# An mLSTM cell with hash routing: the gate prologue in three groups on 32 partitions, with the first rows moved inside SBUF

## The chip, the cores and the metric

The kernel runs on one core of a Trainium2 chip. The metric is the device time of one execution in microseconds; 429.63 us is the median of three runs before the change (429.09 to 429.99). The profile comes from one profiled execution with a span of 427.9 us.

The engines are named as the profile names them: PE (TensorE, with PEld for its weight loads), DVE (VectorE), ACT (ScalarE), POOL (GpSimd) and SP (SyncE). SPq and ACTq are the queues from which SyncE and ScalarE issue DMA transfers; both issue in program order.

## The reference: what is computed

Two blocks follow each other. The first is an mLSTM cell over 4 batches, 8 heads, 768 positions and head size 40. Cut to what matters:

```python
for t in range(S):
    m_new  = np.maximum(f_gate[:, :, t] + m, i_gate[:, :, t])
    f_stab = np.exp(f_gate[:, :, t] + m - m_new)
    i_stab = np.exp(i_gate[:, :, t] - m_new)
    m = m_new
    C = f_stab * C + i_stab * outer(v_t, k_t)
    n = f_stab * n + i_stab * k_t
    h = C @ q_t
    y[:, :, t] = sigmoid(o_gate[:, :, t]) * h / max(abs(n @ q_t), 1)
```

The second sends each of the 3072 rows of width 320 to one of 8 experts by a hash of its token id, and applies `relu(x @ w1[e]) @ w2[e]` with 1024 hidden columns.

## The kernel before

The cell is computed in chunks of P = 128 positions: 24 steps `s`, six per batch (`c = s % 6`), each for all 8 heads of a batch. Within a chunk the gates become decays `exp(A_t + e_u)`, where `A` is a running sum of log decays and `e` belongs to the input position. Those sums are formed on TensorE: `L` holds the rows of `e` and `R` the rows of `A`, each split into three bf16 pieces so that their sum has fp32 precision, and one product of the two gives the matrix that is then exponentiated.

```python
def decays(s):                      # PE, then ACT
    R = Rs[s % 2]
    for hf in range(2):
        for i in range(2):
            nc.tensor.matmul(ab[...], lhsT=Ls[b % 2][...], rhs=R[:, i, hf::2, :], ...)
        nc.scalar.activation(w[:, hf], ab[:], AF.Exp)

def weigh(s):                       # DVE: w = scores * decays
    for hf in range(2):
        nc.vector.tensor_tensor(d["w"][:, hf], d["sp"][hf][:], d["w"][:, hf], op=ALU.mult)
```

The prologue computes the gates of all 32 (batch, head) rows. It does so in two groups: `g0` is the first 256 positions on partitions 0 to 31; `g1` is the other 512 positions, folded to 256 columns on partitions 64 to 127. The gates of `g1` are loaded a second time in that layout, and the running maximum `m` is moved over to it by two transfers inside SBUF.

```python
def gates(rows, m0, m1, f, i, eng):
    nc.vector.tensor_add(aP[r], f, m0)
    nc.vector.tensor_sub(aP[r], aP[r], m1)
    nc.gpsimd.tensor_tensor(iP[r], i, m1, op=ALU.subtract)
    nc.vector.tensor_tensor_scan(AP[r], keep[r], aP[r], 0.0, op0=ALU.mult, op1=ALU.add)
    nc.vector.tensor_tensor(r1[r], AP[r], hi(AP[r]), op=ALU.subtract)
    nc.vector.tensor_sub(iP[r], iP[r], AP[r])
    nc.vector.tensor_tensor(r2[r], r1[r], hi(r1[r]), op=ALU.subtract)
    pieces_of(zA, 0, AP, r1, r2, r, eng)      # three bf16 copies
def gates_e(rows, eng): ...                   # r3, r4, three pieces of e into zE
def gates_rest(rows, eng): ...                # aP, exp(A), exp(aP), r1, r2, three more pieces
```

`zA` and `zE` are written to DRAM (`za_d`, `ze_d`), and `load_a(s)` and `load_e(b, groups)` read the rows that a step needs back into `R` and `L`, one head beside the other. `gates_turn` transposes `exp(aP)` into `kw_T`, the factors for the keys. The order of the prologue, cut:

```python
load_k(0); load_q0(0); load_k(1); load_q0(1); load_v(0); load_k(2)
...                                            # four more gate loads on ACT's queue
tables()                                       # constant parts of R and L
scan of m (g0); turn_k(0); turn_q0(0)
load_q0(2); load_o(0); load_v(1); load_o(1); load_v(2); load_o(2)
scores(0)
gates(g0, ...); gates_e(g0, ...); store_a(g0, A); store_e(g0, A)
turn_k(1); turn_q0(1)
scan of m (g1), two transfers of m to the layout of g1
load_a(0, A); load_e(0, [0])
gates_rest(g0, ...); store_x(g0, A)
Rs[1] <- Rs[0]                                 # two transfers, 128 and 256 KB
memsets of v on POOL
load_q(1, 0); load_q(1, 1)                     # batch 1's q, 2 x 480 KB
gates_turn(g0); decays(0); entering(0); load_a(1, A); k_weights(0)
gates(g1, ...); weigh(0); load_k(3); load_q0(3)
gates_e(g1, ...); store_a, store_e; gates_rest(g1, ...); store_x
...
```

Then the 24 steps. Every engine takes its work in this order:

```python
for s in range(NT):
    load_k(s + 3) (and load_q0(c + 3) in batch 0); load_v(s + 3)
    load_q(b + 2, ...) in chunks 2 and 4; load_o(...); a slice of the experts' weights
    decayed(s)                                 # POOL: C * decay
    turn_k(s + 2); turn_q0(c + 2) / turn_q(b + 1, r, ...)      # PE, evacuated by ACT
    back(s - 1); finish(s - 1)                 # PE, DVE, POOL
    decays(s + 1)
    if s == 0: load_e(0, [1, 2])
    sigmoid(s) in some steps                   # ACT
    state(s); entering(s + 1)                  # PE, DVE: C, qs
    load_a(s + 2, nc.scalar if s == 0 else nc.sync)
    k_weights(s + 1); store of x(s - 1)
    scores(s + 1); weigh(s + 1)
    pad_q(...)                                 # DVE
    for piece in before.get(s, []): piece()    # routing constants and the like
    attend(s)                                  # PE, evacuated by ACT
    if s == 0: sigmoid(0); gates_turn(g1)
    for piece in after.get(s, []): piece()
```

`turn_q` spreads the transposes of the next batch's q over the steps; `first_turns = {1: (0,), 2: (1,), 3: (2,), 4: (3, 4), 5: (5,)}` says which falls into which step of batch 0. `before[0]` holds three iotas with their casts on POOL, `before[1]` the other five. After the steps the rows are gathered from DRAM by expert, and the two layers follow.

Of the kernel before, what the change touches and what calls it, by code (L numbers as in the profile page):

```python
# [8 lines left out]
F32 = mybir.dt.float32  # L9
# [8 lines left out]
P = 128  # L18
NEG = -1e30
# [3 lines left out]
def kernel(  # L23
# [90 lines left out]
    za_d = nc.dram_tensor("decay_pieces", (3 * BH, 6, 2 * P), BF16, kind="Internal").ap()  # L114
    ze_d = nc.dram_tensor("input_pieces", (3 * BH, 3, 2 * P), BF16, kind="Internal").ap()

    with tc.tile_pool(name="gates", bufs=1) as gp, \
# [24 lines left out]
        at = [0, 2 * BH, 3 * BH]  # L142
        fP, iP, aP, AP, r1, r2, r3, r4 = (
            gp.tile([P, W2], F32, name=name) for name in ("fP", "iP", "aP", "AP", "r1", "r2", "r3", "r4")
        )
        mP = gp.tile([P, W2 + 1], F32, name="mP")
        keep = gp.tile([P, W2], F32, name="keep")
        zA = gp.tile([P, 6, W2], BF16, name="zA")
        zE = gp.tile([P, 3, W2], BF16, name="zE")
# [36 lines left out]
        def load_e(b, gs):  # L186
            src = ze_d.rearrange("(g b h) i t -> b (h i) g t", g=NC2, h=H)[b]
            nc.scalar.dma_start(
                Ls[b % 2][: 3 * H, :].rearrange("r (g t) -> r g t", t=W2)[:, gs[0] : gs[-1] + 1],
                src[:, gs[0] : gs[-1] + 1],  # L190
            )

        def load_a(s, eng):
            b, c = s // NB, s % NB
            r0 = c // 2 * BH + b * H
            n = 3 if c == 0 else 6
            src = za_d[r0 : r0 + H, :n, c % 2 * P : (c % 2 + 1) * P].rearrange("h i t -> i h t")
            for i in range(2):
                eng.dma_start(Rs[s % 2][32 : 32 + n, i], src)
# [5 lines left out]
        def pieces_of(z, i0, t, ra, rb, r, eng):  # L205
            for j, piece in enumerate((hi(t[r]), hi(ra[r]), rb[r])):
                if eng[j] is nc.scalar:
                    nc.scalar.copy(z[r, i0 + j, :], piece)
                else:
                    nc.gpsimd.tensor_copy(z[r, i0 + j, :], piece)  # L210

        def gates(rows, m0, m1, f, i, eng):

            r = rows
            first = r.start == 0
            nc.vector.tensor_add(aP[r], f, m0)
            nc.vector.tensor_sub(aP[r], aP[r], m1)
            if first:
                nc.vector.memset(aP[r, 0:1], 0.0)
            nc.gpsimd.tensor_tensor(iP[r], i, m1, op=ALU.subtract)  # L220
            nc.vector.tensor_tensor_scan(AP[r], keep[r], aP[r], 0.0, op0=ALU.mult, op1=ALU.add)
            nc.vector.tensor_tensor(r1[r], AP[r], hi(AP[r]), op=ALU.subtract)
            nc.vector.tensor_sub(iP[r], iP[r], AP[r])
            nc.vector.tensor_tensor(r2[r], r1[r], hi(r1[r]), op=ALU.subtract)
            pieces_of(zA, 0, AP, r1, r2, r, eng)

        def z_rows(r):
            return slice(0, BH) if r.start == 0 else slice(BH, 3 * BH)

        def gates_e(rows, eng):  # L230
            r = rows
            nc.vector.tensor_tensor(r3[r], iP[r], hi(iP[r]), op=ALU.subtract)
            nc.vector.tensor_tensor(r4[r], r3[r], hi(r3[r]), op=ALU.subtract)
            pieces_of(zE, 0, iP, r3, r4, r, eng)

        def store_a(r, eng):
            eng.dma_start(za_d[z_rows(r), :3, :], zA[r, :3, :])

        def store_e(r, eng):
            eng.dma_start(ze_d[z_rows(r)], zE[r])  # L240

        def store_x(r, eng):
            eng.dma_start(za_d[z_rows(r), 3:, :], zA[r, 3:, :])

        def gates_rest(rows, eng):
            r = rows
            Ac = AP[r].rearrange("p (c t) -> p c t", t=P)
            n = r.stop - r.start
            nc.vector.tensor_tensor(
                aP[r].rearrange("p (c t) -> p c t", t=P), iP[r].rearrange("p (c t) -> p c t", t=P),  # L250
                Ac[:, :, P - 1 : P].to_broadcast([n, 2, P]), op=ALU.add,
            )
            nc.scalar.activation(fP[r], AP[r], AF.Exp)
            nc.scalar.activation(aP[r], aP[r], AF.Exp)
            nc.vector.tensor_tensor(r1[r], fP[r], hi(fP[r]), op=ALU.subtract)
            nc.vector.tensor_tensor(r2[r], r1[r], hi(r1[r]), op=ALU.subtract)
            pieces_of(zA, 3, fP, r1, r2, r, eng)

        def gates_turn(rows):
            r = rows  # L260
            n = r.stop - r.start
            tp = ps.tile([P, 2, n], F32, name="tpg", tag="tr", bufs=4)
            for c in range(2):
                nc.tensor.transpose(tp[:, c, :], aP[r, c * P : (c + 1) * P], ident[r, r])
            lo, hi_ = (0, 1) if r.start == 0 else (1, 3)
            nc.vector.tensor_copy(
                kw_T[:, :, lo:hi_, :].rearrange("p c g n -> p c (g n)"), tp[:],
            )
# [325 lines left out]
        def route_index():  # L594
# [7 lines left out]


        before = {
            0: [lambda: iota_consts(0, 3)], 1: [lambda: iota_consts(3, 8)], 2: [route_consts, route_sel],
# [4 lines left out]
        after = {4: [route_counts], **{13 + i: [lambda i=i: route_table(i)] for i in range(NT // TH)}}  # L610
# [3 lines left out]
        first_turns = {1: (0,), 2: (1,), 3: (2,), 4: (3, 4), 5: (5,)}  # L614
# [26 lines left out]
        flat = {id(t): src.rearrange("b h s -> (b h) s") for t, src in ((f_sb, f_gate), (i_sb, i_gate), (fP, f_gate), (iP, i_gate))}  # L641
        nc.scalar.dma_start(f_sb[:], flat[id(f_sb)])
        nc.scalar.dma_start(i_sb[:], flat[id(i_sb)])
# [9 lines left out]
        for i in (1, 2):  # L653
            for t in (fP, iP):
                nc.scalar.dma_start(t[at[i] : at[i] + BH, :], flat[id(t)][:, i * W2 : (i + 1) * W2])
        nc.vector.memset(m_sb[:, 0:1], 0.0)
        tables()
        for t in [ks[2], kws[0]]:
            nc.gpsimd.memset(t[:, :, D:], 0.0)
        nc.vector.memset(keep[:], 1.0)  # L660
        nc.vector.memset(keep.rearrange("p (c t) -> p c t", t=P)[:, :, 0:1], 0.0)
        g0, g1 = slice(0, BH), slice(2 * BH, 4 * BH)
        A, G = nc.scalar, nc.gpsimd
        nc.vector.tensor_tensor_scan(
            m_sb[:, 1 : W2 + 1], f_sb[:, :W2], i_sb[:, :W2], NEG, op0=ALU.add, op1=ALU.max,
        )
        turn_k(0)
        turn_q0(0)
        load_q0(2)
        load_o(0)  # L670
        load_v(1)
        load_o(1)
        load_v(2)
        load_o(2)
        scores(0)
        gates(g0, m_sb[:, :W2], m_sb[:, 1 : W2 + 1], f_sb[:, :W2], i_sb[:, :W2], (G, G, G))
        gates_e(g0, (A, A, A))
        store_a(g0, A)
        store_e(g0, A)
        turn_k(1)  # L680
        turn_q0(1)
        nc.vector.tensor_tensor_scan(
# [310 lines left out]
```

## Time and profile before

| | |
|---|---|
| time, median of three runs | 429.63 us |
| span of the profiled run | 427.9 us |
| PE busy | 386.1 us (90%) |
| DVE, ACT, POOL busy | 136.1, 134.6, 118.7 us |
| DMA moved | 51.37 MB, mean 120 GB/s |
| the 24 steps end (last attend) | at about 164 us |

The profile page gives busy time per engine, the span in 40 slices with a digit for the busy share (9 is 90% or more), the clock that TensorE was granted, the share of the DMA engines, and the chain of work that ended last. Other views give the same trace by stretches of time, by waits (who waited for whom), and in order of time. A wait with several causes is put down to the one that came last. In a line of the timeline or of the chain the first number is the start in us and the second the length.

### The profile page before, as it was taken

The page shows a single profiled execution, that of the slowest core. Times are in us where ns is not written, and L with a number is a line of the kernel's source. Part 1 is how long each engine was busy: PE and PEld are TensorE (multiplying, and loading weights), DVE is VectorE, ACT ScalarE, POOL GpSimd, SP SyncE. Part 2 cuts the span into 40 slices and gives each one's busy share as a digit, 9 for nine tenths or more (in the row PEclk, how much of TensorE's full clock was granted, in tenths as well). Part 3 has the DMA queues.
Part 4 walks back from the last instruction along what each step waited for, and adds up shares of the span by engine and source line. Part 5 has one row for each costly group of instructions (what it writes and reads, how often), then busy time and mean ns, then how long its engine had stood idle before and what let it go on. Part 6 is the DMA issues. An engine that isn't in the chain of part 4 may idle for free.

```text
span 427.9 us, 7402 instructions
## 1 busy us (share of the span) xinstructions
PE 386.1 (90%) x2862; PEld 258.5 (60%) x2862; DVE 136.1 (32%) x371; ACT 134.6 (31%) x238; POOL 118.7 (28%) x204
## 2 busy tenths in 40 slices
PE   2369999999999992599999999999999999999992
PEld 2257867877887871356656557556556566575551
DVE  7464748766675761211020120110110210201100
ACT  5158776686495471011010110110111111111010
POOL 6363323313323422710321501302302312021021
PEclk9868999999999998589999999999999999999997
DMA  8929998899676720527616318235216201000000
GB/s 168 213 61 172 206 218 180 190 205 214 149 161 129 161 90 33 163 96 239 193 46 212 120 29 271 62 98 170 75 64 214 61 8 38 0 15 31 1 17 30
DMA packets 111784, 51.37 MB, mean 120 GB/s; under 512 B 86624, under 2 KB 105892, under 8 KB 111748
## 3 DMA queue, kind: packets, MB, share of 16 engines
q1 hardware_dynamic: 105898, 39.31, 38.2%
q0 software_dynamic: 2496, 8.20, 6.0%
q10 hardware_dynamic: 3354, 3.37, 2.4%
q8 instruction: 23, 0.38, 0.4%
q14 instruction: 13, 0.11, 0.1%
HBM read 42.00 MB, written 8.63 MB: 118 GB/s over the span
## 4 chain that ended last, share of the span: by engine, by line
PE 78%; issue 5%; ACT 5%; DMA 4%; POOL 2%; DVE 1%; SPq 1%; ACTq 0%; POOLq 0%; DVEq 0%
PE mh L834 22%; PE zp L863 21%; PE mh L827 6%; PE sp L351 6%; PE ht L409 6%; PE ht L402 3%; PE ab L311 2%; PE tr L275 2%; PE xo L424 2%; PE ht L382 2%; PE tk L588 1%; PE tp L810 1%; ACT qT L289 1%; PE xb L323 1%; PE tr L288 1%
## 5 line engine op out<-in xcount | busy, mean ns | idle before, releaser
L863 PE MATMUL zp<-w2t,h 128*128 128x320 f32 x384 | 105.2, 433 | 0.0
L834 PE MATMUL mh<-xT,w1t 128*128 128x416 f32 x256 | 98.9, 531 | 0.9 <-POOL xT L896 0.9
L863 PEld LDWEIGHTS zp<-w2t,h 128*128 128x128 f32 x384 | 72.7, 190 | 32.1 <-issue 3.3
L834 PEld LDWEIGHTS mh<-xT,w1t 128*128 128x128 f32 x256 | 47.8, 194 | 44.0 <-issue 41.6
L816 DVE COPY xT<-tp 128x384 f32<-128x384 f32 x16 | 8.9, 558 | 142.3 <-PE tp L812 124.7
L797 POOL DMA_INDIRECT out_dram<-zo,s_idx x26 | 25.6, 986 | 92.5 <-ACT zo L796 92.5
L843 ACT ACTIVATE h<-mh 128x416 f32<-128x416 f32 x32 | 16.6, 517 | 110.1 <-PE mh L827 60.3
L796 ACT COPY zo<-zp 128x320 f32<-128x320 f32 x26 | 11.1, 426 | 101.1 <-PE zp L863 92.9
L841 DVE TENSOR_SCALAR h<-mh 128x416 f32<-128x416 f32 x32 | 18.9, 592 | 53.4 <-PE mh L834 26.9
L359 DVE TENSOR_TENSOR w<-sp,w 128x512 f32<-128x512 f32 x48 | 30.9, 686 | 13.8 <-PE sp L351 10.3
L440 POOL TENSOR_TENSOR x<-x,den 128x320 f32<-128x320 f32 x24 | 17.4, 724 | 64.0 <-DVE den L439 34.1
L351 PE MATMUL sp<-qT,kT 64*128 64x128 f32 x384 | 29.7, 297 | 4.1 <-ACT qT L289 4.1
L351 PEld LDWEIGHTS sp<-qT,kT 64*128 64x128 f32 x384 | 24.9, 199 | 10.8 <-ACT qT L289 6.0
L315 ACT ACTIVATE w<-ab 128x512 f32<-128x512 f32 x48 | 26.6, 611 | 5.0 <-PE ab L311 4.9
L409 PE MATMUL ht<-w,v 128*64 128x128 f32 x384 | 27.1, 285 | 0.0
L827 PE MATMUL mh<-xT,w1c 64*128 64x416 f32 x128 | 26.7, 535 | 0.0
L938 POOL COPY hrem<-h 128x256 f32<-128x256 f32 x8 | 3.2, 400 | 84.1 <-ACT h L843 84.1
L790 POOL DMA_INDIRECT xg<-x_rows,g_idx x24 | 23.4, 976 | 9.7 <-issue 9.7
L417 ACT COPY hT<-ht 128x512 f32<-128x512 f32 x24 | 14.1, 587 | 31.2 <-PE ht L409 31.2
L409 PEld LDWEIGHTS ht<-w,v 128*64 128x64 f32 x384 | 21.2, 140 | 4.0 <-issue 3.1
L289 ACT COPY qT<-tr 128x512 f32<-128x512 f32 x24 | 22.9, 975 | 0.6 <-PE tr L288 0.3
L275 PE MATMUL tr<-ident,k 128*128 128x128 f32 x96 | 17.2, 307 | 4.3 <-DMA k<-in_k_dram 4.3
(177 smaller groups left out, 407.0 us busy)
## 6 DMA issues: line engine op xcount, KB each, us to landing
w2t<-in_moe_w_dram SPq DMA_DIRECT2D x28, 320.0 KB
w1t<-in_moe_w_dram SPq DMA_DIRECT2D x28, 256.0 KB
k<-in_k_dram SPq DMA_DIRECT2D x24, 160.0 KB
v<-in_v_dram SPq DMA_DIRECT2D x24, 160.0 KB
og<-in_o_gate_dram SPq DMA_DIRECT2D x24, 160.0 KB
x_rows<-x SPq DMA_DIRECT2D x24, 160.0 KB
ql<-in_q_dram SPq DMA_DIRECT2D x6, 480.0 KB
w1c<-in_moe_w_dram SPq DMA_DIRECT2D x14, 128.0 KB
```

What stands on the lines that cost most here:

```text
L275: nc.tensor.transpose(tp[:, j, :], d["k"][:, 2 * j : 2 * j + 2, :].rearrange("p h d -> p (h d)"), ident[:])
L289: nc.scalar.copy(qb[b]["T"][:, :, cols], tp[:])
L315: nc.scalar.activation(w[:, hf], ab[:], AF.Exp)
L351: nc.tensor.matmul(sp[hf][:, j, :], lhsT=d["kT"][r, j, :], rhs=q_of(s)[r, j, :], start=True, stop=True,)
L359: nc.vector.tensor_tensor(d["w"][:, hf], d["sp"][hf][:], d["w"][:, hf], op=ALU.mult)
L409: nc.tensor.matmul(place(j, hf), lhsT=d["v"][:, 2 * j + hf, :], rhs=d["w"][:, hf, j, :], start=(c == 0 and j0 == 0), stop=True, skip_group ...
L790: nc.gpsimd.indirect_dma_start(out=xg, out_offset=None, in_=x_d[:, :], in_offset=bass.IndirectOffsetOnAxis(ap=idx, axis=0),)
L797: ins = nc.gpsimd.indirect_dma_start(out=out[:, :], out_offset=bass.IndirectOffsetOnAxis(ap=idx, axis=0), in_=zo[:], in_offset=None, bound ...
L827: nc.tensor.matmul(hp[i][:, :cols], lhsT=w1c[r, fp, :], rhs=xT[r, 2, :cols], start=first, stop=not first,)
L834: nc.tensor.matmul(hp[i][:, :cols], lhsT=w1t[:, db, fb * P : (fb + 1) * P], rhs=xT[:, db, :cols], start=(first and db == 0), stop=(not fir ...
L841: nc.vector.tensor_relu(h[:, 2 * fp, :cols], hp[i][:, :cols])
L863: nc.tensor.matmul(zp[:], lhsT=h[:, fb, j * P : (j + 1) * P], rhs=w[2][:, fb, :], start=(fb == 0), stop=(fb == FB - 1),)
```

## The change

The prologue is rewritten. The gates are now computed in three groups of 256 positions, all on partitions 0 to 31, so that neither the second load of the gates nor the transfers of `m` are needed. The rows of the first step do not go through DRAM: `zA` and `zE` are moved by nine small transfers straight into `R` and `L`. The second group's work stands partly in the prologue and partly in step 0, the third group's in steps 0 to 2, with its exponents and stores behind the evacuations of those steps. Fourteen spare products (`spin`) stand in TensorE's order in the prologue. Loads of `o` and of batch 1's q move to later places, and the first turns of batch 1's q begin a step later. The purpose is an earlier start of the steps. The diff, cut to its core:

```diff
-        fP, iP, aP, AP, r1, r2, r3, r4 = (gp.tile([P, W2], ...) ...)
+        fP, iP, AP, r1, r2, r3, r4 = (gp.tile([BH, W2], ...) ...)
+        aP = [gp.tile([BH, W2], F32, name=f"aP{i}") for i in range(2)]
-        zA = gp.tile([P, 6, W2], BF16, name="zA")
-        zE = gp.tile([P, 3, W2], BF16, name="zE")
+        zA = gp.tile([BH, 6, S], BF16, name="zA")
+        zE = gp.tile([BH, 3, S], BF16, name="zE")
 ...
+        def gates_m(g):     # scan of m for group g (DVE)
+        def gates_a(g):     # two DVE, iP on POOL, scan of A (DVE)
+        def gates_b(g, eng):  # five DVE, six pieces: zA on POOL, zE on eng
+        def gates_end(g):   # one DVE
+        def gates_exp(g, end):  # ACT: exp(aP) if end, else exp(A)
+        def gates_x(g):     # two DVE, three pieces on POOL
+        def store_a(g, eng):  # all six rows of zA;  store_e: three of zE
+        def spin(n):
+            t = ps.tile([P, 2, 512], F32, name="ht")
+            for _ in range(n):
+                nc.tensor.matmul(t[:, 1, :P], lhsT=ident[:], rhs=ident[:], start=True, stop=True)
 ...
+        def gates_last():
+            gates_exp(2, True)
+            gates_x(2)
+            store_a(2, nc.sync)
+            store_e(2, nc.sync)
         before = {
-            0: [lambda: iota_consts(0, 3)], 1: [lambda: iota_consts(3, 8)], 2: [...],
+            0: [lambda: gates_m(2), lambda: gates_a(2), lambda: iota_consts(0, 3)],
+            1: [lambda: gates_b(2, G), lambda: gates_end(2), lambda: iota_consts(3, 8)], 2: [...],
-        after = {4: [route_counts], ...}
+        after = {1: [gates_last], 4: [route_counts], ...}
-        first_turns = {1: (0,), 2: (1,), 3: (2,), 4: (3, 4), 5: (5,)}
+        first_turns = {2: (0,), 3: (1,), 4: (2, 3), 5: (4, 5)}
 ...
-        for i in (1, 2):
-            for t in (fP, iP):
-                nc.scalar.dma_start(t[at[i] : at[i] + BH, :], flat[id(t)][:, i * W2 : (i + 1) * W2])
         tables()
+        nc.vector.memset(Rs[1][32:HB], 0.0)      # was on POOL, later
+        spin(6)
         turn_k(0); turn_q0(0)
+        gates_m(0); gates_a(0); gates_exp(0, False); gates_b(0, A)
         load_q0(2); load_v(1)
+        for j in range(3):
+            for i in range(2):
+                nc.sync.dma_start(Rs[0][32 + j : 33 + j, i], zA[:H, j, :P])
+        for j in range(3):
+            nc.scalar.dma_start(Ls[0][j : 3 * H : 3, :W2], zE[:H, j, :W2])
+        gates_end(0); gates_exp(0, True); gates_x(0)
         turn_k(1); turn_q0(1)
+        store_a(0, A)
 ...     memsets of v
+        scores(0); spin(8)
+        gates_m(1); gates_turn(0); gates_a(1); k_weights(0); gates_b(1, G); gates_end(1)
         Rs[1] <- Rs[0]
+        load_o(0); load_k(3); load_q0(3); load_v(2); load_o(1); load_o(2)
         decays(0); entering(0); load_a(1, A)
+        gates_exp(1, False); weigh(0); gates_x(1); store_e(0, nc.sync)
 ...     in the steps:
+            if s < 2:
+                load_q(1, s)
-            if s == 0:
-                load_e(0, [1, 2])
+            if s == 2:
+                load_e(0, [2])
 ...         after entering(s + 1):
-                if s + 2 < NT:
-                    load_a(s + 2, nc.scalar if s == 0 else nc.sync)
+                if 0 < s < NT - 2:
+                    load_a(s + 2, nc.sync)
+                if s == 0:
+                    gates_exp(1, True); store_a(1, A); store_e(1, A)
+                if s == 1:
+                    gates_exp(2, False)
                 k_weights(s + 1)
 ...         after attend(s):
             if s == 0:
+                load_e(0, [1]); load_a(2, A)
                 sigmoid(0)
-                gates_turn(g1)
+                gates_turn(1)
+            if s == 2:
+                gates_turn(2)
```

(Calls that stand on lines of their own are joined by semicolons here, bodies of the new helpers are told in their comments, and renamings are left out.)

## The prediction

> **What bounds the kernel now.** I read the page first, then the busy time by stretches, the chain in order of time, the waits, and the timelines of the engines up to 65 us.
>
> ```profile
> span 427.9 us, 7402 instructions
> PE 386.1 (90%) x2862; PEld 258.5 (60%) x2862; DVE 136.1 (32%) x371; ACT 134.6 (31%) x238; POOL 118.7 (28%) x204
> ...
> PE   2369999999999992599999999999999999999992
> ...
> PEclk9868999999999998589999999999999999999997
> DMA  8929998899676720527616318235216201000000
> ```
>
> TensorE is full from the fourth slice on (a slice is 10.7 us) except at the hand-over to the experts, which the change leaves alone. So only the first three or four slices can be won, and the gain is whatever a fixed event after them moves by.
>
> ```profile
> 0.00:20.70 20.70, 6.57 (x34) 5.07 (x34) 11.77 (x28) 7.87 (x13) 9.66 (x25) 0.92 0.93 197
> 20.70:24.10 3.40, 3.37 (x15) 2.06 (x17) 1.00 (x3) 1.65 (x4) 2.79 (x12) 0.50 0.33 55
> 27.50:34.40 6.90, 5.62 (x40) 4.51 (x40) 3.91 (x9) 3.67 (x9) 4.57 (x16) 0.51 0.45 91
> 41.00:53.00 12.00, 11.98 (x175) 9.68 (x174) 8.29 (x25) 9.65 (x15) 4.43 (x12) 1.00 0.99 208
> ```
>
> Columns are the stretch, its length, busy PE, PEld, DVE, ACT and POOL, granted clock, DMA share and GB/s. Before 34 us the clock is at half for long stretches and the DMA engines are nearly idle (0.33 to 0.45); from 41 us both TensorE and the DMA engines are full.
>
> ```profile
> 10.28 2.55 DMA decay_pieces<-zA
> ...
> 12.89 3.03 DMA R<-R
> ...
> 24.27 1.30 DVE w L359 x2
> ...
> 28.14 0.59 ACT kT L276
> ...
> 29.42 2.01 PE sp L351 x16
> 31.43 1.93 PE ht L409 x16
> ...
> 39.78 1.02 PE ht L409 x16
> ```
>
> This is the chain (start, length, what). `attend(0)` ends at 33.4 us, `attend(1)` at 40.8; after that the steps cost about 6 us (attend ends at 46.85, 52.8, 59.7, 65.2). The same 16 products take 1.93 us at 31 us and 1.02 at 40: the slow clock.
>
> ```profile
> PE ab L311 <- DMA L<-input_pieces: 2.9, 1, 2.9
> ...
> PE xb L323 <- ACT kT L276: 3.7, 1, 3.7
> ...
> DVE iP L223 <- POOL iP L220: 2.4, 1, 2.4
> ```
>
> These are the waits of the prologue: the first decay products wait for rows that go to memory and back (pieces finished at 10.7 us, rows usable at 20.7); the second step's k copy on ScalarE sits behind the later groups' exponents; VectorE waits for a GpSimd subtraction queued behind memsets.
>
> **What the Trainium skill says.** *TensorE: Matmul & The Clock Gate*, Part 1: the clock starts at half, becomes full after about 3.4 us of sustained work and falls back after an idle window. The trace agrees: the half clock of 27.5 to 34.4 is 6.9 us, two such windows, following 24.1 to 27.5 with TensorE busy only 0.98 us. *DMA: Bandwidth & Descriptors*, Anatomy of one DMA: semaphore waits are on the issuing sequencer, the DMA engines only consume their queues. So a store that waits for its data also holds every load behind it; the trace shows SyncE's queue waiting 3.1 us at one k load. Same page, Queues, rings and completion order: each engine takes a ring in order, and alternates between rings. The trace agrees: a 12 KB row load issued at 16.31 while two 480 KB loads were under way was usable at 20.7, against about 1.1 us for `load_a(1)` in the idle stretch at 22.5. *ScalarE: Activation LUTs*, What ACT_TABLE_LOAD costs: 1283 ns per load; each one here takes 1.28 us.
>
> **Part 1: start of the chain, removed 7 us.** The gate loads land as before (scan at 5.07), and the VectorE operations of group 0 on 32x256 keep their 0.4 to 0.7 us, so zA and zE are again complete at 10.3 and 10.6. What goes is the way through memory. Four gate loads leave ScalarE's queue, so its table copies (4.69 to 8.81) end nearly 3 us earlier and are out of the way. The six moves into R and the three into L are small; issuing takes about 0.3 us each (the small row loads here), so the last are issued at 11.0 and 11.6; with 2.0 us to land (the 2.04 of the second zA store) the first decays can run at 13.7 instead of 20.7. The spin products and earlier transposes keep TensorE busy from 4 to 12.6, so those decays are fast.
>
> **Part 2: attend(0), about 8 us earlier.** The next gate is `load_a(1)`, which still goes through memory. Its store waits for the exponent's pieces (GpSimd 12.0; ScalarE then has two copies of 0.59) and is issued at 13.2, landed at 16; the two loads are issued by 17, in competition with 384 KB of R-to-R and 960 KB of k, q, v, o (sizes from the list of DMA issues, at some 230 GB/s), which keep the rings busy to about 17.5. I take 19.3 for the rows. TensorE idles about 4 us before it, so step 0 is partly at half clock: 1.0 decays, 0.7 state, 0.6 xb, 2.0 scores, 1.9 attend, 6.2 at most. attend(0) ends at about 25, against 33.4. `weigh(0)` (VectorE behind gates_b(1), about 19) is not the last.
>
> **Part 3: attend(1), 7.4 us earlier.** Group 1's stores are issued at about 22 and land at 25; then, after attend(0)'s copy (25.6), ScalarE issues load_e and load_a(2) to 26.6, does the sigmoid with its table (2.3) and copies k (0.6): decays(2) at 29.5. Before, from decays(2) (36.81) to the end of attend(1) (40.8) is 4.0. So attend(1) ends at about 33.4: **-7.4**. One step's latency has become longer than before (8.4 against 7.4).
>
> **Part 4: what group 2 gives back in steps 1 to 3.** gates_b(2) runs on VectorE behind weigh(2), which ends about with attend(1) (call it A): pad 0.3, five operations of about 0.5, gates_end 0.5: A+3.3. GpSimd's sixth piece ends at A+3.5, the five iotas with their casts take 2.0 (38.35 to 40.35 in the trace), the last three pieces 1.5 more: A+7.0. Only then can SyncE issue store_a(2), and **all loads of step 2 stand behind it in SyncE's order**, at about A+7.8. Before, the first of them was issued at 39.67, which is A-1.1.
>
> ```profile
> 39.67 0.85 SPq L161 DMA_DIRECT2D k<-in_k_dram  x1
> ...
> 41.89 0.83 SPq L184 DMA_DIRECT2D ql<-in_q_dram  x1
> 42.77 1.12 SPq L177 DMA_DIRECT2D og<-in_o_gate_dram  x2
> 43.94 2.13 SPq L199 DMA_DIRECT2D R<-decay_pieces  x1
> ```
>
> k, q, v and two o are 800 KB (4 us at 200 GB/s), q of batch 2 480 KB (1.6 us at the 310 GB/s of 16 to 19 us), and `load_a(4)`, last in the ring, lands about A+14. decays(4) to the end of attend(3) is 4.1 (48.67 to 52.77), so attend(3) would end at A+18.1 instead of A+12.0: 6.1 given back. This is the longest chain of guesses here; if the pieces take 0.4 instead of 0.5 us, or the short loads run faster on empty rings, it is 3. I count **+4.4**.
>
> **Part 5: shifted turns.** Batch 1's turns begin a step later, so step 5 has two. scores(6) needs the last qT copy: the chain had ScalarE's L289 at 61.42 and scores at 62.46. One more such copy (0.975 us): **+1.0**. The extra VectorE and GpSimd work in steps 0 to 2 (about 2.3, 3 and 1 us) otherwise lies beside TensorE, since attend(s) needs only qs and w of the step before. The rest of the kernel moves rigidly.
>
> Sum: -7.4 + 4.4 + 1.0 = -2.0, so 429.6 - 2.0 = **427.6 us**.
>
> **Rivals.** (a) *Nothing is given back*: the stores of group 2 come early enough, or step 2's loads have slack. Then only -7.4 + 1.0 and some clock: about 423. For it: steps 1 to 5 have data loaded about three steps ahead; against it: load_a is needed one step after its issue. (b) *The DMA engines become the bound*: by attend(1) batch 1's q (960 KB, 4 us) has not been loaded ahead as it was before 20 us, and the share from 34 us is already 1.0. With the late step 2 this puts everything back and more: 430 to 433. (c) *GpSimd becomes the bound of steps 1 and 2*: its nine pieces plus iotas delay the decayed state (0.46), which the state addition of step 2 waits for; perhaps 1 us more, 428.6.
>
> **Range and chances.** attend(1) is uncertain by 2.5 us either way (free phase of the clock window, landing of load_a(1)), the give-back by 3. Together about 4: **422.0 to 432.5**, from just below (a) to the top of (b). Faster by over 2% needs below 421.0, more than the whole of part 3: 0.10. Slower by over 2% means above 438.2, which would need a stall larger than the gain plus 8: 0.04. Within 2%: 0.86.
>
> **What would show it.** First L311 at 13 to 15 us; attend(0) ending at 23 to 26; attend(1) at 32 to 35. Then a hole in the DMA row and in SyncE's issues between about A and A+8, ended by GpSimd's zA, followed by decays(4) waiting for R from memory: right if attend(3) ends at 49 to 53, wrong if it ends near 46. Two qT copies ahead of scores(6) confirm part 5. I am wrong outright if attend(1) is not ahead by at least 5 us, or if later steps, after attend(5), differ from before.

## The result, and the profile after

The changed kernel takes 436.13 us (median; 435.15 to 436.78) against 429.69 us for the kernel before on the same chip: ratio **1.015, interval 1.0127 to 1.0172**. It became slower by 1.5%, where 427.6 us and a range up to 432.5 had been predicted.

The page after, with the rows that answer to those shown before:

```profile
span 435.0 us, 7495 instructions
...
PE 394.4 (91%) x2892; PEld 265.5 (61%) x2892; DVE 143.1 (33%) x385; ACT 133.8 (31%) x236; POOL 124.1 (29%) x217
...
PE   8548699999999997299999999999999999999992
...
PEclk9687889999999999579999999999999999999997
DMA  7774689779857651244913526316207101000000
```

A slice is now 10.9 us. TensorE starts full (8 where it was 2) but is at 4 to 8 up to the fifth slice, where it was at 9 from the fourth on. The clock is below full up to the sixth slice. DMA has a 4 in the fourth, where the kernel before had 9. The busy time by stretches says the same; the columns are as before, and the last stretch is an extra one:

```profile
0.00:20.70 20.70, 14.45 (x94) 11.90 (x95) 16.67 (x37) 11.36 (x20) 14.27 (x41) 0.83 0.73 139
20.70:24.10 3.40, 3.22 (x28) 2.48 (x27) 1.96 (x6) 0.21 (x1) 2.98 (x9) 0.51 0.52 103
27.50:34.40 6.90, 1.88 (x15) 1.06 (x17) 1.42 (x6) 3.71 (x5) 1.88 (x6) 0.74 0.81 153
41.00:53.00 12.00, 8.15 (x89) 6.34 (x88) 6.58 (x21) 6.12 (x11) 7.61 (x26) 0.86 0.53 112
39.00:49.00 10.00, 8.02 (x92) 6.39 (x88) 7.64 (x21) 4.32 (x9) 8.74 (x28) 0.83 0.20 42
```

TensorE does 14.45 us of work before 20.7 (before: 6.57), and then only 1.88 us from 27.5 to 34.4 (before: 5.62) and 8.15 of 12 us from 41 to 53 (before: 11.98, at full clock and DMA share 0.99). From 39 to 49 the DMA engines are nearly idle.

How far each step has come, by the end of its `attend` (us):

| | before | predicted | after | after minus before |
|---|---|---|---|---|
| first decays | 20.7 | 13.7 | 14.4 | -6.3 |
| attend(0) | 33.3 | 25 | 24.9 | -8.4 |
| attend(1) | 40.8 | 33.4 | 39.1 | -1.7 |
| attend(2) | 46.9 | | 48.6 | +1.7 |
| attend(3) | 52.8 | 49.8 | 60.4 | +7.6 |
| attend(5) | 65.2 | 63.2 | 73.2 | +8.0 |
| last attend | 163.7 | | 171.7 | +8.0 |

(49.8 and 63.2 are the prediction's sums applied to the column before: -7.4 + 4.4, and 1.0 more.) Everything is lost between attend(0) and attend(3): 6.7 us in step 1, 3.4 in step 2, 5.9 in step 3. After attend(5) the two kernels move alike.

Who waits up to 65 us, in the kernel after (total, times, longest):

```profile
PE ab L324 <- DMA R<-decay_pieces: 10.3, 3, 5.6
...
ACT L356 <- DMA L<-input_pieces: 4.5, 1, 4.5
...
ACT dec L342 <- DVE qs L340: 3.3, 1, 3.3
...
PE ab L324 <- ACT kT L289: 1.7, 1, 1.7
```

L324 is the decay product (L311 before). The wait of the first decays for L, 2.9 us before, has shrunk to 0.64, but the same product now waits three times for R, the rows that go through memory. In order of time on TensorE:

```profile
32.46 1.67 PE L324 MATMUL ab<-R,L 128*64 128x512 bf16 x4 [5.58 <-DMA R<-decay_pieces]
...
35.29 2.08 PE L364 MATMUL sp<-qT,kT 64*128 64x128 f32 x16
...
42.76 0.88 PE L324 MATMUL ab<-R,L 128*64 128x512 bf16 x4 [1.72 <-ACT kT L289]
...
54.94 1.13 PE L324 MATMUL ab<-R,L 128*64 128x512 bf16 x4 [3.38 <-DMA R<-decay_pieces]
```

The brackets hold the idle time just before and what ended it: 5.58 us ahead of decays(2), 3.38 ahead of decays(4). After the first, the 16 score products take 2.08 us, the slow clock.

ScalarE in step 1 shows where decays(2) gets its rows:

```profile
24.21 0.16 ACT L342 COPY dec<-xb 128x4 f32<-128x4 f32 x1 [3.30 <-DVE qs L340]
...
24.27 0.60 ACTq L265 DMA_DIRECT2D decay_pieces<-zA  x1
24.92 0.62 ACTq L269 DMA_DIRECT2D input_pieces<-zE  x1
...
29.02 0.31 ACTq L188 DMA_DIRECT2D L<-input_pieces  x1
29.44 1.14 ACTq L195 DMA_DIRECT2D R<-decay_pieces  x2
30.66 1.28 ACT L356 ACT_TABLE_LOAD   x1 [4.50 <-DMA L<-input_pieces]
```

Group 1's stores leave ScalarE's queue at 24.27 and 24.92, behind the small copy `dec`, which waited 3.30 us for VectorE. They land at 28.73 and 29.00, and only then can the loads be issued (29.02 on); the rows land at 32.3 and 32.8. Meanwhile ScalarE stands idle for 4.5 us behind its own issues.

SyncE's queue shows the hole of step 2:

```profile
36.05 0.35 SPq L454 DMA_DIRECT2D x_rows<-x  x1
45.20 0.58 SPq L265 DMA_DIRECT2D decay_pieces<-zA  x1
45.83 0.60 SPq L269 DMA_DIRECT2D input_pieces<-zE  x1
46.48 0.59 SPq L160 DMA_DIRECT2D k<-in_k_dram  x1
...
48.39 0.75 SPq L183 DMA_DIRECT2D ql<-in_q_dram  x1
...
50.45 2.63 SPq L195 DMA_DIRECT2D R<-decay_pieces  x2
```

Nothing is issued between 36.4 and 45.2. Then come group 2's stores, all loads of step 2, and last, at 50.45, `load_a(4)`. It lands at 54.8 and 55.0, and decays(4) starts at 54.94.

### The profile page after: what moved, and what is told of

Read it like the earlier page. It is cut to its first block, busy times and chain, and to the rows that moved or that the text cites. A ratio compares the mean times of both kernels' runs of the same rounds, so it can differ in the third digit from the quotient of the medians.

```text
span 435.0 us, 7495 instructions
## 1 busy us (share of the span) xinstructions
PE 394.4 (91%) x2892; PEld 265.5 (61%) x2892; DVE 143.1 (33%) x385; ACT 133.8 (31%) x236; POOL 124.1 (29%) x217
## 4 chain that ended last, share of the span: by engine, by line
PE 51%; issue 5%; POOL 2%; DMA 1%; POOLq 0%; DVE 0%
PE mh L860 22%; PE zp L889 21%; PE mh L853 6%; PE tp L836 1%; PE zp L930 1%; POOL out_dram L823 1%; DMA xr<-x_rows,g_idx 1%; POOL xg L816 1%; PE tp L838 1%; DMA x_rows<-x 0%; POOL x L453 0%; DVE h L867 0%; POOLq L969 0%; POOLq L823 0%; POOL hrem L964 0%
## 5 line engine op out<-in xcount | busy, mean ns | idle before, releaser
L453 POOL TENSOR_TENSOR x<-x,den 128x320 f32<-128x320 f32 x24 | 17.3, 722 | 64.2 <-DVE den L452 33.6
L364 PE MATMUL sp<-qT,kT 64*128 64x128 f32 x384 | 30.9, 305 | 0.8 <-ACT qT L302 0.8
L324 PE MATMUL ab<-R,L 128*64 128x512 bf16 x96 | 18.6, 428 | 13.8 <-DMA R<-decay_pieces 11.0
L364 PEld LDWEIGHTS sp<-qT,kT 64*128 64x128 f32 x384 | 25.9, 206 | 7.5 <-issue 5.2
```

What stands on the lines that cost most here:

```text
L324: nc.tensor.matmul(ab[i * HB : (i + 1) * HB], lhsT=Ls[b % 2][:, c * P + i * HB : c * P + (i + 1) * HB], rhs=R[:, i, hf::2, :], start=True, ...
L364: nc.tensor.matmul(sp[hf][:, j, :], lhsT=d["kT"][r, j, :], rhs=q_of(s)[r, j, :], start=True, stop=True,)
```

## The experiments

Four came first, each on one term of the prediction; later ones add up what had worked and test what was left. The ratio is always to the kernel before on the same chip, as chips differ by some tenths of a per cent. Step times come from one profiled execution each; in four kernels whose work up to that point is the same (the changed one, e1_order, e5_order_exp, e7_order_turns) attend(1) ended at 39.1, 38.4, 39.6 and 39.1, so a difference there of up to 1.2 us between two kernels can be chance.

**e1_order: group 2's stores behind step 2's loads.** The stores leave `gates_last` and are issued after the loads of step 2 and ahead of `load_a(4)`:

```diff
         def gates_last():
             gates_exp(2, True)
             gates_x(2)
-            store_a(2, nc.sync)
-            store_e(2, nc.sync)
 ...     step s, after the loads of k, q, v and o:
+            if s == 2:
+                store_a(2, nc.sync)
+                store_e(2, nc.sync)
```

> The changed kernel with group 2's two stores moved in SyncE's order from ahead of step 2's loads to behind them (ahead of load_a(4)); nothing else. Theory, the order of the queue: the loads go out at about 38 us instead of 46.5, the stores at 45.2 as now, load_a(4) lands at about 49.5 instead of 55.0, decays(4) starts at about 51.6 instead of 54.9 and attend(3) ends at 55 to 56 instead of 60.4: about 431.5 us. Rival, GpSimd's pieces or the total bytes are the bound: decays(4) stays at 54 to 55 and the time within 1 us of 436.1.

Measured: 430.65 us, ratio 1.0043 (1.0025 to 1.006), so about 4.6 of the 6.4 us are back (1.07% of 430). attend(3) ends at 54.2 instead of 60.4. SyncE's queue in this kernel:

```profile
36.67 0.43 SPq L160 DMA_DIRECT2D k<-in_k_dram  x1
...
44.64 0.58 SPq L265 DMA_DIRECT2D decay_pieces<-zA  x1
45.27 0.60 SPq L269 DMA_DIRECT2D input_pieces<-zE  x1
46.87 0.64 SPq L195 DMA_DIRECT2D R<-decay_pieces  x2
```

The stores are issued about as late as in the changed kernel (44.64 against 45.20); what differs is what stands behind them. The loads of step 2 have gone ahead, and `load_a(4)` is issued at 46.87 and lands 1.6 and 1.8 us later, instead of at 50.45 with 4.4 us to land. decays(4) starts at 50.2, and no longer waits for its rows. The order of issue on one queue is the larger part of the loss.

**e2_warm: 24 spin products ahead of decays(2).**

```diff
+            if s == 1:
+                spin(24)
             if s + 1 < NT:
                 decays(s + 1)
```

> The changed kernel with 24 spare products ahead of decays(2), in TensorE's idle stretch of step 1 (26.9 to 32.4 us). Theory, the clock: step 1 then runs at full clock, the way from decays(2) to the end of attend(1) shrinks from 6.7 to about 4 us, and all later work, which hangs on weigh(2), comes 1.6 to 2.6 us earlier: 433.5 to 434.5 us. Rival, step 1 is bound by ScalarE (table loads and exponents): under 0.7 us.

Measured: 434.65 us, 1.0133 (1.0107 to 1.0158), by the interval not told apart from the changed kernel's 1.015; the 1.6 to 2.6 us that were expected did not come. From decays(2) to the end of attend(1) it takes 4.0 us instead of 6.7: exactly the 4.0 of the kernel before. So 2.7 us of step 1 are the slow clock. But the spins end late (decays(2) at 33.5 instead of 32.5), and attend(3) ends at 60.3, where it was: decays(4) waits for its rows all the same (3.79 us).

**e3_early: group 1's last exponent and stores issued ahead of ScalarE's copy of the state's decay.**

```diff
+            if s == 0:
+                gates_exp(1, True); store_a(1, A); store_e(1, A)
             state(s)
             if s + 1 < NT:
                 entering(s + 1)
-                if s == 0:
-                    gates_exp(1, True); store_a(1, A); store_e(1, A)
```

> The changed kernel with group 1's last exponent and its two stores ahead of entering(1) in ScalarE's order, so that they don't wait for the copy of dec (24.2 us). Theory, the way through memory: the stores go out at 22.2 instead of 24.3, ahead of the 480 KB q load, land at about 25.3 instead of 29.0, the row loads go out right after attend(0)'s copy at 26.2, decays(2) starts at about 29.5 instead of 32.5: attend(1) and all after it 2.5 to 3 us earlier, 433 to 433.6 us. Rival, landing is set by the traffic whenever they are issued: they land at 28 or later, and under 1 us is won.

Measured: 434.02 us, 1.0134 (1.0095 to 1.0174), by the interval not told apart from the changed kernel either; what the edit does is read from the profile, and its worth from e6_order_early below. ScalarE's queue in this kernel:

```profile
22.48 0.60 ACTq L265 DMA_DIRECT2D decay_pieces<-zA  x1
23.13 0.62 ACTq L269 DMA_DIRECT2D input_pieces<-zE  x1
24.49 0.16 ACT L342 COPY dec<-xb 128x4 f32<-128x4 f32 x1 [3.03 <-DVE qs L340]
...
25.75 0.31 ACTq L188 DMA_DIRECT2D L<-input_pieces  x1
26.17 0.80 ACTq L195 DMA_DIRECT2D R<-decay_pieces  x2
```

The stores go 1.8 us earlier and land 2.2 and 2.0 us after issue instead of 4.4 and 4.1: they are now ahead of batch 1's 480 KB q load (issued at 23.88; in the changed kernel at 23.37, ahead of the stores). But now the row loads stand behind it: issued at 25.75 to 26.48, they land at 30.2 to 31.3, after 4.5 to 4.9 us. decays(2) starts at 31.2 and attend(1) ends at 36.9, 2.2 us earlier than in the changed kernel; the last attend ends 2.8 us earlier.

**e9_q_late: the 480 KB loads out of the way.** The changed kernel with batch 1's two q loads issued behind `load_a(3)`, batch 2's one step later:

```diff
-            if s < 2:
-                load_q(1, s)
+            if s in (3, 5):
+                load_q(2, s // 2 - 1)
-            if c in (2, 4) and b + 2 < B:
+            if b and c in (2, 4) and b + 2 < B:
                 load_q(b + 2, c // 2 - 1)
 ...
                     load_a(s + 2, nc.sync)
+                    if s == 1:
+                        load_q(1, 0); load_q(1, 1)
 ...
-        first_turns = {2: (0,), 3: (1,), 4: (2, 3), 5: (4, 5)}
+        first_turns = {3: (0, 1), 4: (2, 3), 5: (4, 5)}
```

> The changed kernel, with batch 1's two 480 KB q loads issued behind the row loads of step 3 instead of ahead of the loads of steps 0 and 1 (and batch 2's a step later; its turns begin at step 3, two to a step). Theory (the round trip of group 1's rows is long because its packets share the rings with a 480 KB load): issued at the same time, about 24.3, the two stores land in 2.0 to 2.5 us instead of 4.4 and 4.1, decays(2) starts at 29.5 to 30.5 instead of 32.5, attend(1) ends near 36.5 instead of 39.1; of this little is left at the end, since load_a(4) still stands behind group 2's stores: time 433.5 to 435. Rival (a round trip of this size takes some 4 us under any load, or the time is lost before the issue): landing 4 us or more, decays(2) after 32, no change of the time: 435.5 to 437.

Measured: 434.27 us, 1.0103 (1.0076 to 1.0129). Issued at 24.40 and 25.04, the stores land after 3.1 and 3.5 us: between the two theories. The q load ahead of them thus cost 1.4 and 0.6 us. Loads of 160 KB are still in the rings; that they make up the rest, down to the 2.0 us of e1_order's stores, was not tested. decays(2) starts at 31.9, attend(1) ends at 37.9. More came in step 3 than was expected (attend(3) 55.9 instead of 60.4): with batch 2's q load no longer ahead of it, `load_a(4)` has landed at 51.9 instead of 55.0, 6.6 us after the first load of the step instead of 8.5, and the step behind it then runs at the full clock (4.1 us instead of 5.5).

**e4_sbuf_rows: the moves inside SBUF alone, in the kernel before.** The nine moves of the change take the place of `load_a(0, A)` and `load_e(0, [0])`, ahead of `store_a(g0, A)`:

```diff
+        for j in range(3):
+            for i in range(2):
+                nc.sync.dma_start(Rs[0][32 + j : 33 + j, i], zA[:H, j, :P])
+        for j in range(3):
+            nc.scalar.dma_start(Ls[0][j : 3 * H : 3, :W2], zE[:H, j, :W2])
         store_a(g0, A); store_e(g0, A)
 ...
-        load_a(0, A)
-        load_e(0, [0])
```

> The kernel before with one part of the change alone: the first step's rows moved from zA and zE straight into R and L (six moves on SyncE, three on ScalarE) instead of read back from memory; group 0's store stays for the later steps. If the first rows' way through memory was what held step 0: decays(0) at about 15.5 instead of 20.7, attend(0) at 30 to 31 instead of 33.3, about 427 us. Rival: step 0 is held by the second group's work ahead of it on VectorE, GpSimd and ScalarE (xb behind the k copy at 28.1): decays(0) comes earlier, attend(0) within 1 us of 33.3, 429 us.

Measured: 428.56 us, 0.9993 (0.9979 to 1.0006): no gain. TensorE in this kernel, after its first decays:

```profile
18.04 1.61 PE L311 MATMUL ab<-R,L 128*64 128x512 bf16 x4 [0.73 <-DMA R<-zA]
...
25.93 1.31 PE L311 MATMUL ab<-R,L 128*64 128x512 bf16 x4 [4.38 <-DMA R<-decay_pieces]
...
28.33 0.64 PE L323 MATMUL xb<-R,Lx 128*64 128x512 bf16 x2 [0.28 <-ACT kT L276]
28.90 2.08 PE L351 MATMUL sp<-qT,kT 64*128 64x128 f32 x16
```

The first decays are only 2.7 us earlier than before (18.0; SyncE issues six moves at 0.63 to 0.82 us each behind the o and v loads), the second wait for rows from memory, and the xb products then for the same ScalarE copy as before, at 28.3; attend(0) ends at 32.9, as the rival said. The second rows even come later than before (25.9 instead of 23.7): batch 1's two 480 KB q loads now go out behind the six moves, at 18.8 and 19.4 instead of 13.5 and 14.9, and `load_a(1)`, behind them, takes 4.2 us to land instead of 1.7. A short way for the first rows is worth nothing here while the second rows and the later groups' work hold step 0. That leaves the reordering of the prologue as what made attend(0) early; it was not tested alone.

**e6_order_early: e1_order and e3_early together.**

> e1_order and e3_early together: group 2's stores behind step 2's loads, and group 1's stores ahead of entering(1). The two losses lie one after the other, so they should add: attend(1) at about 36.9 as in e3_early, everything after it 1.5 to 2 us ahead of e1_order: 428.5 to 429 us. Rival, the DMA engines are full and what is won at attend(1) is lost again at load_a(4): as e1_order, 430.6 us.

Measured: 429.13 us, 0.9974 (0.9958 to 0.9991), faster than the kernel before by a little. attend(1) 36.0, attend(3) 50.8, attend(5) 64.2 (before: 40.8, 52.8, 65.2). From e1 to e6 the ratio falls by 0.7%, about 3 us, with intervals that do not touch: that is what the earlier stores of group 1 are worth once the order of step 2 is mended, and it is what e3's profile had shown (2.8 us at the last attend).

The next kernels stand on top of e1 or e6.

**e5_order_exp: e1_order with group 2's last exponent behind decays(3)**, since in the changed kernel decays(3) waits 1.72 us behind it.

```diff
         def gates_last():
-            gates_exp(2, True)
             gates_x(2)
 ...
             if s == 2:
+                gates_exp(2, True)
                 load_e(0, [2])
```

> e1_order, with group 2's last exponent moved in ScalarE's order from ahead of step 2's k and q copies to behind decays(3). Theory: in e1_order ScalarE waits 2.2 us at that exponent for VectorE's gates_end and so holds the k copy, for which TensorE waits 1.9 us ahead of decays(3); without it decays(3) starts at about 40.4 instead of 42.2 us and attend(2) ends at 45 to 46 instead of 48.0; load_a(4) landing at 49 then sets step 3, so about 1 us of the time: 429.5 us. Rival, GpSimd's late decay of the state sets step 2: attend(2) stays at 48.

Measured: 432.16 us, 1.0039 (1.0015 to 1.0064), the same as e1_order. decays(3) comes 1.9 us after attend(1) instead of 3.8, but attend(2) ends at 48.1 as in e1 (48.0): the rival came true. TensorE waits for the state `C`, that is for VectorE, and VectorE for GpSimd:

```profile
45.99 0.33 DVE L401 TENSOR_TENSOR C<-C,ht 128x164 f32<-128x164 f32 x1 [2.02 <-POOL C L381]
...
46.37 0.67 PE L415 MATMUL ht<-qs,C 64*64 64x128 f32 x16 [2.43 <-DVE C L401]
```

GpSimd comes to the decay of the state (L381) only behind group 2's pieces and the five iotas. The stores of group 2, too, still go 6 us after attend(1), and the rows land at 50.0 and 50.2, just ahead of decays(4) at 50.3.

**e7_order_turns: e1_order with batch 1's turns spread otherwise**, `first_turns = {2: (0,), 3: (1, 2), 4: (3, 4), 5: (5,)}`, so that step 5 has one.

> e1_order with batch 1's q turned in chunks 2, 3, 3, 4, 4, 5 instead of 2, 3, 4, 4, 5, 5, so that step 5 has one turn. Prediction's part 5: step 5 is then 0.9 to 1.0 us shorter and step 3 no longer, 429.7 us. Rival: the turn costs the same wherever it is, 430.6 us.

Measured: 432.38 us, 1.0066 (1.0044 to 1.0088), not better than e1_order. Step 5 takes 5.6 us instead of 6.5, and step 3 takes 7.1 instead of 6.2: a turn costs about 0.9 us in whichever of these steps it stands.

**e8_all: e6_order_early with the edits of e5 and e7, 14 spins and the five iotas moved to step 3.**

> The changed kernel with all the mendings: group 2's stores behind step 2's loads, its last exponent behind decays(3), group 1's stores ahead of entering(1), 14 spare products in step 1's hole, five iotas moved from step 1 to step 3, step 5 with one turn. If the waits named are all there is, attend(1) ends at 35.5 to 36.5, attend(2) at 42 to 43, attend(3) at 48 to 49 (before: 52.8), and the time is 425 to 426 us, faster than the kernel before. Rival, the DMA engines are the bound from 34 us on: attend(3) not below 51.5, and at best the time of the kernel before.

Measured: 430.08 us, 1.001 (0.9988 to 1.0032), no better than e6, where 425 to 426 had been expected. attend(1) and attend(2) are early (34.8 and 42.6, in e6 36.0 and 44.3), but decays(4) starts at 48.8 (in e6 46.5). The trace names two things. `store_a(2)` goes out at 40.88 behind batch 2's 480 KB q load (38.15) and lands after 5.1 us; and ScalarE, which issues `load_e(0, [2])`, stands 7.7 us until `store_e(2)`, issued behind it, has landed at 46.1. The rival's sign is there (attend(3) at 53.6, the time of the kernel before), but the DMA engines' share from 41 to 53 us is 0.72: they are not full. The next kernels answer these two waits.

**e10_no_ring: e6_order_early with the iotas in step 3, `load_e(0, [2])` on SyncE's queue, and batch 2's q load a step later.**

> The kernel with the order of step 2 and the early exponent of group 1 (429.13, 0.9974 of before), and in step 2: the five iotas with casts off GpSimd's way to group 2's last pieces (2.1 us, moved to step 3), the row load of L for group 2 on SyncE's queue instead of ScalarE's (ScalarE stood 3.3 us behind it), batch 2's 480 KB q load a step later. Theory (decays(4) waits for one chain: pieces on GpSimd, store, row load): store issued at 39.5 to 40 instead of 41.8, landed in 2.1, decays(4) at 44 to 44.5 instead of 46.5, attend(3) 48.5 to 49 instead of 50.8; ratio to before 0.992 to 0.994. Rival (TensorE is full there anyway, or the loads are given back later, as they come no sooner): attend(3) earlier but attend(6) not: 0.997.

Measured: 428.54 us, 0.9974 (0.9959 to 0.9988), the same as e6, where 0.992 to 0.994 had been expected. The stores come 4.5 us after attend(1) instead of 5.8, land in 2.2 and 2.0, and the rows of decays(4) are there at 46.4. But decays(4) starts at 48.4, as TensorE isn't ready: in this execution step 2 ran at the slow clock (its 16 score products took 2.08 us, attend(2) ended at 46.4; in e6 at 44.3). With ScalarE's exponent still ahead of decays(3), TensorE is idle for 1.87 us there. The two profiles are not of a kind: 430.70 us is among the longest of e10's times (426.93 to 431.25), and e6's 427.46 the shortest of its own.

**e11_sum: e10_no_ring with e5's and e9's edits.**

> The same, with group 2's last exponent behind decays(3) and batch 1's q loads behind the row loads of step 3. Theory: decays(2) at 28.5 instead of 30.4 and attend(1) at 34 instead of 36.0; decays(4) at 43, attend(3) at 47.5 (before the change 52.8); ratio 0.986 to 0.990 (425 at this chip's 430). Rival (bytes, not waits, set steps 2 to 5: all loads of these steps have to pass by then anyway): attend(3) early but attend(5) not below 62, ratio 0.995 or more.

Measured: 426.66 us, 0.9938 (0.9915 to 0.9962). attend(1) 35.4, attend(2) 42.1, decays(4) 44.9, attend(3) 49.2, attend(5) 62.6. Faster than before by 0.6%, where 1.0 to 1.4% was expected: the early steps came within 1.9 us of what was named, with step 1 still at the slow clock (5.9 us from decays(2) to attend(1)). Of the rival's signs one is there, attend(5) not below 62, the ratio of 0.995 or more is not.

**e12_sum_warm: the same with `spin(14)` ahead of decays(2).**

> The same, with 14 spin products ahead of decays(2), so that step 1 runs at the full clock. Theory: attend(1) 1 to 1.5 earlier than without them, attend(3) as much, ratio 0.983 to 0.987. Rival (decays(4) waits for rows whose time the clock of step 1 doesn't set): same as without spins within 0.2%, or above it.

Measured: 426.79 us, **0.9925 (0.9908 to 0.9942)**; not told apart from e11 by the intervals, and 0.13% from it, as the rival said; the 0.983 to 0.987 of the theory did not come. TensorE in this kernel (the view begins at 28 us and so shows the last 18 of the spins' 28 matmuls, two for each product):

```profile
27.76 2.17 PE L281 MATMUL ht<-ident 128*128 128x128 f32 x18
29.86 0.62 PE L324 MATMUL ab<-R,L 128*64 128x512 bf16 x4
...
31.08 1.16 PE L364 MATMUL sp<-qT,kT 64*128 64x128 f32 x16
...
44.24 0.89 PE L324 MATMUL ab<-R,L 128*64 128x512 bf16 x4 [0.80 <-DMA R<-decay_pieces]
```

The score products take 1.16 us (2.08 in the changed kernel), attend(1) ends at 33.9, and decays(4) waits 0.80 us instead of 3.38. Against e11, attend(1) is 1.5 us earlier, attend(3) 0.7, and the last attend 0.4 later (161.9 and 161.4). The same stretch of busy time, 27 to 41 us, first in the changed kernel:

```profile
27.00:41.00 14.00, 8.48 (x86) 6.47 (x87) 6.39 (x17) 6.54 (x10) 4.87 (x14) 0.76 0.69 143
```

and in e12_sum_warm:

```profile
27.00:41.00 14.00, 12.69 (x183) 10.57 (x182) 11.37 (x29) 9.42 (x17) 10.48 (x29) 1.00 0.98 208
```

Full clock, and a DMA share of 0.98 instead of 0.69. This version is faster than both kernels: than the one before by 0.75% (interval above), than the changed one by some 2.2%, worked out from the two ratios as 0.9925 / 1.015.

Not all of the lead lasts. e12 is ahead of the kernel before by 3.5 us at attend(5) (61.7 against 65.2), by 2.5 at attend(7), and by 1.8 from attend(13) to the last (161.9 against 163.7). The 1.7 us go in steps 6, 7 and 11, 12. There (60 to 75 and 88 to 104 us) e12's decay products wait 2.1 us in all for rows from memory, those of the kernel before 0.3. Why these rows come late was not tested and stays open.

## Why the prediction was wrong, point by point

**Part 1, the start (13.7 predicted, 14.4 measured): right but for 0.7.** An issue of such a move takes 0.63 to 0.82 us, and the first on ScalarE 1.56, where 0.3 had been counted; so the last move into `L` is issued at 12.3 instead of 11.6, and lands after 1.9. That is the 0.7. "So those decays are fast" was wrong: the spins end at 10.6, TensorE is idle for 2.89 us before 13.5, the granted clock is half from 13.8 on, and the products take 1.16 us instead of 0.62.

**Part 2, attend(0) at 25 (24.9): right.** The store went at 13.1 and landed at 16.1, as worked out (13.2 and 16); the second rows came at 18.8, half a microsecond ahead of what was assumed.

**Part 3, attend(1) 7.4 us earlier (1.7 measured): the step that failed first.** "Group 1's stores are issued at about 22 and land at 25 ... decays(2) at 29.5 ... to the end of attend(1) is 4.0". Three terms of it were mis-sized, and together they are the 5.7 us missing at attend(1):
- Issue: 24.27 instead of 22. In ScalarE's order a copy stood ahead of the stores and waited 3.30 us for VectorE; e3_early moved it and the stores went at 22.48.
- Round trip: 4.4 us instead of 3 for the store of A; both stores had landed at 29.0 instead of 25. From there to decays(2) it took 3.5 us, where 4.5 had been counted, so of these 4.0 us 3.0 are left: decays(2) starts at 32.5 instead of 29.5. The Trainium skill, *DMA: Bandwidth & Descriptors*, Anatomy of one DMA, gives about 2.0 us fixed for a DMA that GpSimd issues; of the stores here, issued by ScalarE and SyncE, those with no large load ahead agree (2.0 to 2.2 us in e3_early and e1_order), and behind a 480 KB load the same transfer takes 4.0 to 4.5. The prediction had quoted that rings are shared and then used a number from emptier ones. (Its "about 1.1 us for `load_a(1)`" counts from the end of the issue; from its start, as the 4.4 us beside it does, the two row loads took 1.65 and 1.67.) e3 and e9 show that the time of issue and the load ahead both matter; neither edit alone brings decays(2) to 29.5, both together do (e11: 29.5; its other edits lie behind that point).
- Clock: 6.7 instead of 4.0 us from decays(2) on. The prediction took step 1's length from a stretch at full clock, but its own plan left TensorE idle ahead of decays(2); in the 5.58 us of idling the granted clock fell to half (at 30.8 us, until 37.7), as the Trainium skill, *TensorE: Matmul & The Clock Gate*, Part 1, says of an idle window. e2_warm shows the term by itself: 2.7 us at attend(1). At the end of the kernel nothing of it was seen, neither in e2 nor in e12, as decays(4) waits for its rows.

**Part 4, give-back of 4.4 us (9.3 measured): right mechanism, wrong size.** The hole was there, ended by GpSimd's last pieces, and e1_order shows that the order of the stores and the loads of step 2 is its cause. With A = 39.1, the end of attend(1): last piece A+6.1 (predicted A+7.0), first load A+7.4 (A+7.8), `load_a(4)` landed A+15.9 (A+14), attend(3) A+21.3 (A+18.1). Three terms make the 4.9: from the first load to the landing of the last 8.5 us instead of 6.2 (less 0.4, as the first went earlier; without the 480 KB load e9 still needs 6.6, for which the prediction had 4.6), the step after it 5.5 us at a part of the clock instead of 4.1, and the choice of 4.4 where the working gave 6.1. That cut of 1.7 had no line of the profile behind it; it leaned on empty rings making the loads fast, and it went the wrong way.

**Part 5, the shifted turns (+1.0): right.** Step 5 takes 6.4 us instead of 5.5; e7_order_turns shows that the cost follows the turn, but that nothing is won by moving it.

**The sum.** At attend(5): -1.7 in place of -7.4, +9.3 in place of +4.4, and +0.4 for steps 4 and 5 (-0.5 and +0.9) give +8.0, as measured. Some 0.8 of it comes back after the steps (span +7.2). The prediction had said that it would be wrong outright if attend(1) was not ahead by at least 5 us; that is what happened.

**The rivals.** (a), nothing given back, fell. (b), the DMA engines as the bound, gave the time nearest to the measured one for the wrong reason: from 41 to 53 us their share is 0.53, where the kernel before has 0.99. They are half idle, not full. It is nearer the truth in e12, where the share is 0.98 from 27 to 41 us and 0.81 from 41 to 53; whether bytes bound that kernel was not tested. (c), GpSimd as the bound of steps 1 and 2, was right in kind: its pieces end the hole in the changed kernel, and once ScalarE's exponent is out of the way, step 2 waits for its decay of the state, as (c) had said: 2.43 us in e5. In e12, with the iotas elsewhere, TensorE still waits 1.31 us there for VectorE, but VectorE only 0.3 for GpSimd. What the iotas alone are worth no run shows, since e10 moved them together with two other things.

## What to carry to other kernels

When a dependent pair of transfers, a store and the load that reads it back, stands in front of a step, work out its time with what shares the rings at that moment, and give the clock after the wait its own term. A store put on the queue that also issues the loads holds all of them until its data is ready: put it behind the loads that do not depend on it, and put large loads behind the small ones that the next step needs. A latency cut at the start was worth nothing here (e4_sbuf_rows) until the next such pair was also shorter.

## What the runs showed of the hardware that was not expected

- The same stores (all 32 rows, a third of the columns) land in 2.0 to 2.2 us with no large load ahead (group 2 in the changed kernel and e1_order), in 2.3 to 3.5 beside loads of 160 KB (group 1 in e9, e11, e12), and in 4.0 to 5.1 behind one of 480 KB (group 1 in the changed kernel and e1_order, `store_a(2)` in e8).
- The issue itself stretches: `load_a(4)`'s first row load took 0.29 us to issue in e1_order and 2.28 in the changed kernel behind six loads. What the issue waits for was not tested.
- The granted clock changes only on a fixed grid: in the changed kernel at 13.8, 24.0, 30.8, 37.7, 44.5, 47.9, 54.7 and 58.1 us, always a whole multiple of 3.41 us apart. Where the grid lies differs between executions: with the same work, the full clock came back in step 1 at 37.7, 35.9 and 38.3 us in the changed kernel, e1_order and e5_order_exp, and attend(1) ended at 39.1, 38.4 and 39.6.
- A wait shorter than that grid can bring the slow clock: ahead of decays(3), waits of 1.72 to 1.87 us went with score products of 1.88 to 2.08 us in six profiles (the changed kernel, e1, e2, e7, e9, e10), waits of 1.43 and 1.63 us with 1.16 us (e6, e3). Where between them the limit lies, and what else decides it, was not tested.
